# Batch 0 of a fused linear attention and swish layer, laid out as head half x 64 partitions with nine tokens each

## The chip, the cores and the metric

The kernel runs on one core of a Trainium2 chip. The metric is the device time in microseconds (us) of one execution of the whole program. Below, PE is the matrix engine (its weight loads are listed as PEld), DVE the vector engine, ACT the scalar engine with its function tables, POOL the engine that here issues all loads, and SP the engine that issues the stores and DMA transposes.

## What is computed

Linear attention with phi(x) = elu(x) + 1, and behind it a layer of two products with a swish between them. All inputs are float32.

```python
batch, n_heads, seq, head_dim = (8, 8, 576, 64)
d_model, d_ff = (512, 2048)

def phi(x):
    return np.where(x > 0, x, np.exp(x) - 1.0) + 1.0
q_p, k_p = (phi(q), phi(k))
kv = np.einsum('bhsd,bhse->bhde', k_p, v)
z = np.sum(k_p, axis=2)
num = np.einsum('bhsd,bhde->bhse', q_p, kv)
den = np.einsum('bhsd,bhd->bhs', q_p, z)[..., None] + 1e-06
x = (num / den).transpose(0, 2, 1, 3).reshape(B * S, H * D)

h = x @ w_in
g = h * (1.0 / (1.0 + np.exp(-beta * h)))
out = g @ w_out
```

## The kernel before

Everything is computed in bfloat16 with float32 accumulation; the loads convert on the way. The order of work on each engine is the order of the program text: the kernel switches the framework's own scheduling off and writes the order out by hand. Each engine works through its own list and waits where an operand is not ready or a buffer is not free.

**Batches and row blocks.** The eight batches are worked through one after another. The 576 tokens of a batch are four row blocks of 128 (token 4p + j of the first 512 lies on partition p, as block j) and a tail of 64 tokens, which makes the fifth block (`NT` = 5). The tails of all eight batches are gathered in `xT_tail` and form a ninth pass (`b == B`) at the end.

**Attention of one batch.** `exp_` (L203, ACT), `relu` (L210, DVE) and `phi` (L216 a minimum with 1, L217 an addition, DVE) make phi of k and q. `v_copy` (L299) puts v beside columns of ones, so that one product gives kv and z. `kv_mm` (L274) makes kv, 40 products of 64 stationary columns each, `kv_evac` (L284) moves it into a block-diagonal operand `kv_bd`. q is transposed (`q_trans`, L309, on PE for batches 1 and 2, by DMA from batch 3), then `num_mm` (L328) gives numerator and denominator of a row block and `num_norm` (L342 to L344, DVE) divides. `x_trans` (L362) transposes the result into `xT` for batches 0 to 2, a DMA does so from batch 3.

**The two products.** `h_phase` and `h_last` (`h_mm`, L382) multiply by `w_in`, 16 column blocks `ff` of 128, and `silu` (L374, ACT) follows. `y_phase` or `y_phase_wide` (`y_mm`, L422) multiply by `w_out`, and `y_out` and `store` write the rows out. The attention of batch b + 1 is placed among the products of batch b: a dictionary `plan` says behind which group which steps are recorded. `w_out` is loaded in float32 into buffers that are free at the start, and `w_out_scale` (L186 on DVE, L188 on ACT) multiplies it by 1/beta.

**Batch 0** has nothing to hide behind. Its k, q and v are loaded by `load_halves` in two halves of the heads (L118) with one load of the tail tokens between them (L123). For q, `split0` makes the two summands max(x, 0) and exp(min(x, 0)) (L235 to L237), and `q_add0` (L245) transposes both on PE and adds them in PSUM; `q_out0` moves the sum to `qT`. 32 products without a use (`warm`, L490) run on PE while the first loads are under way. The w_in products of batch 0 take row blocks 0 and 1 one by one at first, as these become ready.

**Loads.** All are issued by POOL, in program order, and served by one queue: k, q, v of batch 0, four quarters of `w_in` (L147), k and q of batch 1 (L73, L77), the first half of `w_out` (L112), and then the third quarter of `w_out`, v of batch 1 and the last quarter. Each issue waits until the load eight places before it has landed. PSUM is two pools: `mm` (four banks) and `att` (two pairs of banks); a step that takes a buffer waits for the reader of the one that had it before.

Of the kernel before, what the change touches and what calls it, by code (L numbers as in the profile page):

```python
# [10 lines left out]
BF16 = mybir.dt.bfloat16  # L11
# [5 lines left out]
def kernel(  # L17
# [24 lines left out]
    WARM = 32  # L42
# [71 lines left out]
    def load_halves(dst, src):  # L114

        for i in range(2):
            hs = slice(i * HH, (i + 1) * HH)
            nc.gpsimd.dma_start(  # L118
                out=dst[:, hs, 0:NJ, :].rearrange("p h j d -> p h (j d)"),
                in_=src[0, hs, 0:MAIN, :].rearrange("h (p j) d -> p h (j d)", j=NJ),  # L120
            )
            if i == 0:
                nc.gpsimd.dma_start(  # L123
                    out=dst[0:TAIL, :, NJ, :],
                    in_=src[0, :, MAIN:S, :].rearrange("h s d -> s h d"),
                )
# [4 lines left out]
    nc.vector.memset(g_sb[0][:, 0, :], 0.0)  # L131
    clear_tail(0)
    nc.vector.memset(vraw[0][TAIL:P, :, NJ, :], 0.0)
# [7 lines left out]
    load_halves(xqk[0][:, 1], k)  # L141
    make_identity(nc, identity)
    make_identity(nc, ident16)
    load_halves(xqk[0][:, 0], q)
    load_halves(vraw[0], v)
    for i in range(4):
        nc.gpsimd.dma_start(out=w_in_sb[i], in_=w_in_v[:, :, i * 512 : (i + 1) * 512])  # L147
    load_k(1)
    load_q(1)
    load_w_out(0)  # L150
    load_w_out(1)
# [7 lines left out]
    for i in range(2):  # L159
        nc.vector.memset(vaug[i][:, :, :, D : D + 2], 1.0)  # L160
        nc.vector.memset(vaug[i][TAIL:P, NJ, :, D : D + 2], 0.0)

# [6 lines left out]

    def make_beta():  # L170
        bps = att_banks()[:, 0, 0:FC]
        nc.tensor.matmul(bps, beta_row, ident16, is_transpose=True, start=True, stop=True)
# [33 lines left out]

    def relu(b, a, h0=0, h1=H):
        if h0 == 0:
            st[b, "r", a] = work.tile([P, H, NT, D], BF16, tag="r", name="r")
        nc.vector.tensor_scalar(  # L210
            st[b, "r", a][:, h0:h1], xqk[b % NX][:, a, h0:h1], 0.0, None, ALU.max
        )

    def phi(b, a, h0=0, h1=H):
        e = st[b, "e", a][:, h0:h1]
        nc.vector.tensor_scalar(e, e, 1.0, None, ALU.min)  # L216
        nc.vector.tensor_add(  # L217
            st[b, "p"][:, a].rearrange("p j (h d) -> p h j d", h=H)[:, h0:h1],
            st[b, "r", a][:, h0:h1], e,
        )  # L220

    def split0(h0, h1):


        if h0 == 0:
            st["r0"] = work.tile([P, H, NT, D], BF16, tag="r", name="r")
            st["e0"] = work.tile([P, H, NT, D], BF16, tag="e", name="e", bufs=3)
        x = xqk[0][:, 0, h0:h1]
        e, r = [
            st[a].rearrange("p h j d -> p (h j d)").rearrange(  # L230
                "p (j h d) -> p h j d", j=NT, h=H
            )[:, h0:h1]
            for a in ("e0", "r0")
        ]
        nc.vector.tensor_scalar(e, x, 0.0, None, ALU.min)  # L235
        nc.scalar.activation(e, e, ACTF.Exp)
        nc.vector.tensor_scalar(r, x, 0.0, None, ALU.max)  # L237

    def q_add0(t, bank, p0, p1):
        n = rows(t)  # L240
        for p in range(p0, p1):
            for src in ("r0", "e0"):
                a = st[src].rearrange("p h j d -> p (h j d)")
                c0 = t * DM + p * P
                nc.tensor.matmul(  # L245
                    bank[:, p * P : p * P + n], a[:n, c0 : c0 + P],
                    identity[:n, :n],
                    start=(src == "r0"), stop=(src == "e0"), skip_group_check=True,
                )

    def q_out0(t, bank, dve):
        n = rows(t)
        copy(
            st[0, "qT"][:, t, :, :n],
            bank.rearrange("p (c n) -> p c n", c=KC)[:, :, :n], dve,
        )
# [152 lines left out]

# [258 lines left out]
```

## Time and profile before

| | |
|---|---|
| median of 6 runs | 300.88 us (300.66 to 301.82) |
| the profiled execution | 300.82 us, of which the span from the first to the last instruction is 299.1 us |
| PE busy | 285.5 us, 95% of the span |
| ACT, DVE, POOL busy | 176.0, 134.1 and 54.5 us |
| DMA | 36.44 MB in 71687 packets, 39264 of them under 512 B |
| first product with w_in, first product with w_out | at 20.93 us, at 36.77 us |

All times inside the execution are microseconds from the start of the span, of the one execution that was profiled. A line of the timeline gives the start, the length, the engine, the source line, the operation with its output and inputs, shapes and count, and in brackets how long the engine had been idle before and what ended that. Busy times of PE are modelled from pipelined matrix products, so a product of 512 columns that is listed with 0.38 us follows the one before it after 0.22 us.

### The profile page before, as it was taken

The numbers are of one execution on the slowest core, as the hardware profiler recorded it, in microseconds if no ns is written. First come the engines' busy times: TensorE is split into PE (matmuls) and PEld (weight loads), VectorE is DVE, ScalarE is ACT, GpSimd is POOL, SyncE is SP. The second block draws the span as 40 slices with busy tenths as digits, with TensorE's granted clock in tenths as the row PEclk, the third lists the DMA queues.
The fourth block names the chain that finished last, engine by engine and source line by source line (L and its number), as shares of the span: only waits on it lengthen the run. The fifth ranks groups of instructions, "written<-read, shape, count | busy, mean of one in ns | idle before, by whom it ended". The sixth has DMA issues, their size and how long they took to land.

```text
span 299.1 us, 4767 instructions
## 1 busy us (share of the span) xinstructions
PE 285.5 (95%) x1882; PEld 146.0 (49%) x1903; DVE 134.1 (45%) x260; ACT 176.0 (59%) x235; POOL 54.5 (18%) x71
## 2 busy tenths in 40 slices
PE   3979998999999999999999999999999999999994
PEld 1458445654556454445444544444444444444444
DVE  6773469703678144824482448244825400110012
ACT  3569894889989690769076907690761067007600
POOL 8943564742201400060002000000000000000000
PEclk9999999999999999999999999999999999999999
DMA  7999999999926996399539243224322710020024
GB/s 83 170 207 196 366 300 195 224 223 192 181 69 164 147 146 123 87 137 197 133 84 120 60 127 84 41 61 124 85 40 62 109 52 1 35 72 35 0 55 88
DMA packets 71687, 36.44 MB, mean 122 GB/s; under 512 B 39264, under 2 KB 66160, under 8 KB 71664
## 3 DMA queue, kind: packets, MB, share of 16 engines
q0 software_dynamic: 40944, 20.45, 48.3%
q1 hardware_dynamic: 30560, 15.55, 21.5%
q8 instruction: 15, 0.25, 0.3%
q10 hardware_dynamic: 160, 0.13, 0.2%
q14 instruction: 8, 0.07, 0.1%
HBM read 36.71 MB, written 9.44 MB: 154 GB/s over the span
## 4 chain that ended last, share of the span: by engine, by line
PE 80%; DMA 11%; DVE 3%; POOL 2%; issue 1%; ACT 1%; POOLq 0%
PE mm L382 36%; PE mm L422 36%; DMA vraw<-in_v_dram 6%; DMA xqk<-in_q_dram 5%; PE att L328 3%; PE att L274 2%; PE mm L454 1%; PE att L382 1%; POOL xqk L118 1%; DVE xs L344 1%; PE att L362 1%; ACT q_pT L301 1%; PE att L309 1%; DVE qk_p L217 1%; POOL xqk L123 0%
## 5 line engine op out<-in xcount | busy, mean ns | idle before, releaser
L422 PE MATMUL mm<-w_out,g 128*128 128x512 bf16 x541 | 127.4, 379 | 1.2 <-issue 0.3
L374 ACT ACTIVATE g<-mm,beta_c 128x512 bf16<-128x512 f32 (+2 forms) x156 | 95.2, 633 | 51.7 <-PE mm L382 51.2
L382 PE MATMUL mm<-xT,w_in 128*128 128x512 bf16 (+2 forms) x560 | 107.5, 349 | 0.5 <-ACT xT L301 0.5
L382 PEld LDWEIGHTS <-w_in 128*128 128x128 bf16 x656 | 62.2, 98 | 61.4 <-issue 0.8
L422 PEld LDWEIGHTS <-g 128*128 128x128 bf16 x560 | 52.7, 98 | 57.0
L432 DVE COPY y_sb<-mm 128x512 f32<-128x512 f32 x27 | 18.7, 692 | 70.6 <-PE mm L422 69.1
L203 ACT ACTIVATE e<-xqk 128x2560 bf16<-128x2560 bf16 (+1 forms) x16 | 34.5, 2196 | 5.1 <-DMA xqk<-in_k_dram 5.1
L374 ACT ACT_TABLE_LOAD x6 | 7.7, 1283 | 38.1 <-PE mm L382 38.0
L344 DVE TENSOR_TENSOR xs<-att,rden 128x512 bf16<-128x512 f32 (+1 forms) x40 | 27.6, 690 | 1.4
L217 DVE TENSOR_TENSOR qk_p<-r,e 128x2560 bf16<-128x2560 bf16 (+1 forms) x16 | 22.5, 1409 | 0.5
L73 POOL DMA_DIRECT2D vraw<-in_v_dram x7 | 6.2, 879 | 79.0 <-DVE vaug L299 72.2
L216 DVE TENSOR_SCALAR e<-e 128x2560 bf16<-128x2560 bf16 (+1 forms) x16 | 12.8, 802 | 14.5 <-ACT e L203 14.5
L284 DVE CAST kv_bd<-att 64x260 bf16<-64x260 f32 x16 | 6.8, 426 | 27.0 <-PE att L274 26.8
L342 DVE TENSOR_SCALAR den<-att 128x8 f32<-128x8 f32 (+1 forms) x40 | 6.4, 161 | 27.4 <-PE att L328 27.4
L328 PE MATMUL att<-kv_bd,q_pT 128*128 128x130 bf16 (+1 forms) x160 | 16.1, 222 | 1.0 <-ACT q_pT L301 0.4
L328 PEld LDWEIGHTS <-q_pT 128*128 128x128 bf16 (+1 forms) x160 | 11.7, 100 | 10.7 <-DVE xs L344 2.1
L210 DVE TENSOR_SCALAR r<-xqk 128x2560 bf16<-128x2560 bf16 (+1 forms) x16 | 12.5, 789 | 7.2 <-DMA xqk<-in_k_dram 4.2
L382 PE MATMUL mm<-xT_tail,w_in 128*128 128x512 bf16 x63 | 13.9, 379 | 0.1
L73 POOL DMA_DIRECT2D xqk<-in_k_dram x7 | 9.2, 1319 | 8.9 <-ACT e L203 6.2
L490 PE MATMUL mm<-g,identity 128*128 128x512 bf16 x33 | 9.5, 453 | 0.2 <-issue 0.2
L299 DVE COPY vaug<-vraw 128x2560 bf16<-128x2560 bf16 (+1 forms) x9 | 7.3, 806 | 4.4 <-DMA vraw<-in_v_dram 4.4
L203 ACT ACT_TABLE_LOAD x7 | 9.0, 1283 | 0.1
(76 smaller groups left out, 150.0 us busy)
## 6 DMA issues: line engine op xcount, KB each, us to landing
out_dram<-y_sb SPq DMA_DIRECT2D x32, 256.0 KB, 2.3
xqk<-in_k_dram POOLq DMA_DIRECT2D x7, 512.0 KB, 11.5
xqk<-in_q_dram POOLq DMA_DIRECT2D x7, 512.0 KB, 12.6
vraw<-in_v_dram POOLq DMA_DIRECT2D x7, 512.0 KB, 11.3
w_in<-in_moe_w_in_dram POOLq DMA_DIRECT2D x4, 512.0 KB, 11.7
g<-in_moe_w_out_dram POOLq DMA_DIRECT2D x4, 512.0 KB, 10.6
xqk<-in_moe_w_out_dram POOLq DMA_DIRECT2D x2, 512.0 KB, 14.8
xT<-in_moe_w_out_dram POOLq DMA_DIRECT2D x2, 512.0 KB, 12.5
```

Source lines behind the costliest of these rows:

```text
L73: eng.dma_start(out=dst[:, :, 0:NJ, :].rearrange("p h j d -> p h (j d)"), in_=src[b, :, 0:MAIN, :].rearrange("h (p j) d -> p h (j d)", j=NJ),)
L203: nc.scalar.activation(st[b, "e", a][:, h0:h1], xqk[b % NX][:, a, h0:h1], ACTF.Exp)
L210: nc.vector.tensor_scalar(st[b, "r", a][:, h0:h1], xqk[b % NX][:, a, h0:h1], 0.0, None, ALU.max)
L216: nc.vector.tensor_scalar(e, e, 1.0, None, ALU.min)
L217: nc.vector.tensor_add(st[b, "p"][:, a].rearrange("p j (h d) -> p h j d", h=H)[:, h0:h1], st[b, "r", a][:, h0:h1], e,)
L328: nc.tensor.matmul(nps[:n, p // 2, c0 : c0 + 2 * (D + 1)], st[b, "qT"][:, t, p, :n], kv_bd[b % 2][:, p], start=True, stop=True, skip_group ...
L344: nc.vector.tensor_mul(xs[:n], nv[:, :, :, 0:D], rden[:n, :, :, None].to_broadcast([n, 2, 4, D]))
L374: nc.scalar.activation(g_sb[b % 2][:, ff, c0:c1], hp[:, c0:c1], ACTF.Silu, scale=beta_c[:, ff : ff + 1],)
L382: nc.tensor.matmul(hp[:, c0:c1], w_in_sb[ff // 4][:, kc, (ff % 4) * P : (ff % 4 + 1) * P], x[:, t0:t1, kc, :] if b < B else x[:, kc, c0:c1 ...
L422: nc.tensor.matmul(yp, g_sb[b % 2][:, ff, t * P : (t + 1) * P], w_out_sb[ff // 4][:, ff % 4, :], start=(ff == 0), stop=(ff == FC - 1),)
L432: nc.vector.tensor_copy(y_sb, yp)
L490: nc.tensor.matmul(st["warm"], identity, g_sb[0][:, 0, :], start=True, stop=True, skip_group_check=True,)
```

## The change

- **Layout of batch 0.** Partitions 0 to 63 hold heads 0 to 3, partitions 64 to 127 heads 4 to 7, and partition p of a half holds tokens 9p to 9p + 8 of each head. There is no tail load. Each load is two DMAs of 64 partitions (`load_nine`). The output rows of batch 0 are stored accordingly, 64 rows at a time.
- **Order of loads.** q's tokens 0 to 3 first, then k, two halves of v, and the other five tokens of q. The first half of w_out is issued ahead of k and q of batch 1.
- **Products of batch 0.** k's and v's product (`kv_mm0`) and q's transposes (`q_trans0`) use 64 of the 128 rows of the array, the two head halves in the two row halves, with outputs in different banks. The transposes of q's second part (`q_second`, `q_tail0`) are placed among the w_in products, and so is the numerator of row block 2.
- **phi** is min(exp(x), max(x, 0) + 1) in all batches: `relu` adds 1 in the same instruction, and one minimum of two tensors takes the place of a minimum and an addition.
- **Warm-up products** are 20 at the start, on an operand that needs no identity matrix, and 8, 2, 3 and 4 between steps of batch 0.
- **beta**: the transpose stays early on PE, its five DVE instructions move between the two copies of v.
- Some steps change engine or place: two `x_trans` copies go from ACT to DVE, memsets for later batches (`tidy0`) go behind batch 0's use of the buffers, `w_out_scale(0)` comes earlier in the plan.

```diff
-    WARM = 32
+    WARM = 20
...
+    def load_nine(dst, src, h0=0, h1=HH, j0=0, j1=N9):
+        for g in range(2):
             nc.gpsimd.dma_start(
+                out=dst[g * TAIL : (g + 1) * TAIL, h0:h1, j0:j1, :].rearrange(
+                    "p h j d -> p h (j d)"
+                ),
+                in_=src[0, g * HH + h0 : g * HH + h1, :, :]
+                .rearrange("h (p j) d -> p h j d", j=N9)[:, :, j0:j1, :]
+                .rearrange("p h j d -> p h (j d)"),
+            )
...
-    load_halves(xqk[0][:, 1], k)
+    load_nine(q9, q, j1=4)
+    load_nine(k9, k)
     make_identity(nc, identity)
     make_identity(nc, ident16)
-    load_halves(xqk[0][:, 0], q)
-    load_halves(vraw[0], v)
+    load_nine(v9, v, h1=2)
+    load_nine(v9, v, h0=2)
+    load_nine(q9, q, j0=4)
     for i in range(4):
         nc.gpsimd.dma_start(out=w_in_sb[i], in_=w_in_v[:, :, i * 512 : (i + 1) * 512])
+    load_w_out(0)
+    load_w_out(1)
     load_k(1)
     load_q(1)
-    load_w_out(0)
-    load_w_out(1)
...
-            st[b, "r", a][:, h0:h1], xqk[b % NX][:, a, h0:h1], 0.0, None, ALU.max
+            st[b, "r", a][:, h0:h1], xqk[b % NX][:, a, h0:h1], 0.0, 1.0, ALU.max, ALU.add
...
-        e = st[b, "e", a][:, h0:h1]
-        nc.vector.tensor_scalar(e, e, 1.0, None, ALU.min)
-        nc.vector.tensor_add(
+        nc.vector.tensor_tensor(
             st[b, "p"][:, a].rearrange("p j (h d) -> p h j d", h=H)[:, h0:h1],
-            st[b, "r", a][:, h0:h1], e,
+            st[b, "r", a][:, h0:h1], st[b, "e", a][:, h0:h1], ALU.min,
         )
...
+    def q_trans0(t, banks, c0):
+        for jj in range(2 if t < NJ else 1):
+            for a in range(2):
+                for g in range(2):
+                    gs = slice(g * TAIL, (g + 1) * TAIL)
+                    m0 = c0 + a * P + jj * TAIL
+                    nc.tensor.matmul(
+                        banks[:, g, m0 : m0 + TAIL],
+                        st["p0"][0][gs, 2 * t + jj, 2 * a : 2 * a + 2, :],
+                        identity[gs, gs],
+                        is_transpose=True, start=True, stop=True, skip_group_check=True,
+                    )
...
+    def kv_mm0(a, kvp):
+        for j in range(N9):
+            for g in range(2):
+                gs = slice(g * TAIL, (g + 1) * TAIL)
+                m0 = a * 2 * (D + 1)
                 nc.tensor.matmul(
+                    kvp[:, g, m0 : m0 + 2 * (D + 1)],
+                    st["p0"][1][gs, j, 2 * a : 2 * a + 2, :],
+                    va9[gs, j, 2 * a : 2 * a + 2, 0 : D + 1],
+                    start=(j == 0), stop=(j == N9 - 1), skip_group_check=True,
                 )
...
     begin(0)
-    make_beta()
     st["warm"] = mm_bank([P, 512])
     warm(WARM)
...
+    beta_trans()
...
+    exp0(0, 0, 4)
+    relu0(0, 0, 4)
+    phi0(0, 0, 4)
+    exp0(1, 0, 5)
+    exp0(1, 5, N9)
+    qb = att_banks(BF16)
+    q_trans0(0, qb, 0)
+    q_trans0(1, qb, 256)
+    warm(8)
+    q_out0(0, qb, 0, False)
+    q_out0(1, qb, 256, False)
+    relu0(1, 0, 5)
+    relu0(1, 5, N9)
+    phi0(1, 0, 5)
+    phi0(1, 5, N9)
+    v_copy0(0, 2)
+    make_beta()
+    kvp = att_banks()
+    kv_mm0(0, kvp)
+    warm(2)
+    v_copy0(2, HH)
+    kv_mm0(1, kvp)
+    kv_evac0(kvp)
+    warm(3)
+    num_mm(0, 0)
+    num_mm(0, 1)
+    exp0(0, 4, N9)
+    relu0(0, 4, N9)
     silu_table()
     num_norm(0, 0)
+    warm(4)
+    x_trans(0, 0, dve=True)
+    phi0(0, 4, N9)
     num_norm(0, 1)
...
         {
-            1: [F(x_trans, 0, 1)],
-            2: [F(num_mm, 0, 3), F(num_norm, 0, 3)],
-            5: [F(x_trans, 0, 2), F(num_mm, 0, 4), F(num_norm, 0, 4)],
-            8: [F(x_trans, 0, 3)],
-            12: [F(x_trans, 0, 4)],
-            17: [F(begin, 1), F(relu, 1, 1)],
-            19: [F(relu, 1, 0), F(w_out_scale, 0)],
+            1: [F(q_second)],
+            3: [F(x_trans, 0, 1, dve=True), F(num_mm, 0, 2), F(num_norm, 0, 2)],
+            5: [F(num_mm, 0, 3), F(num_norm, 0, 3)],
+            6: [F(q_tail0)],
+            7: [F(x_trans, 0, 2)],
+            9: [F(x_trans, 0, 3)],
+            10: [F(num_mm, 0, 4), F(num_norm, 0, 4), F(tidy0)],
+            14: [F(x_trans, 0, 4)],
+            17: [F(w_out_scale, 0)],
+            19: [F(begin, 1), F(relu, 1, 1), F(relu, 1, 0)],
         },
```

## The prediction

> **What bounds the kernel now.** I read the page first, then the busy times by stage, then the first 21 us and the stretch from 43 to 51 us instruction by instruction. The stages (stretch and its length, then busy us of PE, PEld, DVE, ACT, POOL, granted clock, DMA share, GB/s):
>
> ```profile
> 4.50:20.93 16.43, 14.31 (x131) 7.98 (x133) 11.65 (x30) 9.01 (x11) 12.29 (x15) 1.00 1.35 177
> 20.93:26.58 5.65, 5.58 (x72) 4.85 (x72) 2.81 (x8) 5.18 (x15) 1.90 (x3) 1.00 1.31 203
> 26.58:36.70 10.12, 10.12 (x65) 6.06 (x65) 3.76 (x7) 9.15 (x16) 5.40 (x7) 1.00 1.30 306
> 44.00:57.00 13.00, 11.45 (x125) 6.67 (x125) 11.44 (x25) 8.07 (x14) 6.89 (x9) 1.00 1.53 205
> 57.00:254.00 197.00, 195.79 (x1259) 97.15 (x1272) 91.18 (x167) 124.23 (x157) 20.61 (x24) 1.00 0.66 112
> ```
>
> After 20.93 us, where the first product with w_in starts, PE is busy all the time but for 1.55 us between 44 and 57 us and some 1.2 us in the 197 us behind. So a change can win only two things: an earlier 20.93, and that 1.55. Whatever it adds to PE behind 20.93 is paid in full. Every DVE instruction that it takes from batches 2 to 7 (the minimum in phi, 0.84 us each) is worth nothing by itself: DVE is busy 91 of 197 us there, PE 195.8.
>
> The head, from the timeline (start, length, instruction):
>
> ```profile
> 6.09 1.27 ACT L203 ACTIVATE e<-xqk 128x1280 bf16<-128x1280 bf16 x1 [3.85 <-DMA xqk<-in_k_dram]
> 8.57 1.27 ACT L203 ACTIVATE e<-xqk 128x1280 bf16<-128x1280 bf16 x1 [1.21 <-DMA xqk<-in_k_dram]
> 10.40 0.83 DVE L217 TENSOR_TENSOR qk_p<-r,e 128x1280 bf16<-128x1280 bf16 x1
> 14.43 0.49 DVE L299 COPY vaug<-vraw 128x1280 bf16<-128x1280 bf16 x1 [1.16 <-DMA vraw<-in_v_dram]
> 15.68 0.70 DVE L299 COPY vaug<-vraw 128x1280 bf16<-128x1280 bf16 x1 [0.76 <-DMA vraw<-in_v_dram]
> 16.44 0.51 PE L274 MATMUL att<-vaug,qk_p 128*64 128x65 bf16 x20 [0.96 <-DVE vaug L299]
> 16.98 0.87 DVE L284 CAST kv_bd<-att 64x260 bf16<-64x260 f32 x2 [0.60 <-PE att L274]
> 18.00 0.40 PE L328 MATMUL att<-kv_bd,q_pT 128*128 128x130 bf16 x4 [0.28 <-ACT q_pT L301]
> 20.93 0.61 PE L382 MATMUL mm<-xT,w_in 128*128 128x128 bf16 x8 [0.45 <-ACT xT L301]
> ```
>
> The second half of v, landing at 15.68, ends last; k was there at 8.57. Behind v everything is a chain: copy, 20 products, eviction, numerator, normalisation, transpose, first product with w_in. And the later stall:
>
> ```profile
> 43.77 1.15 DVE L299 COPY vaug<-vraw 128x2560 bf16<-128x2560 bf16 x1 [2.46 <-DMA vraw<-in_v_dram]
> 44.84 0.97 DVE L216 TENSOR_SCALAR e<-e 128x2560 bf16<-128x2560 bf16 x1
> 45.16 0.82 PE L274 MATMUL att<-vaug,qk_p 128*64 128x65 bf16 x40 [0.46 <-ACT g L374]
> 45.85 1.49 DVE L217 TENSOR_TENSOR qk_p<-r,e 128x2560 bf16<-128x2560 bf16 x1
> 47.40 0.62 PE L309 MATMUL att<-identity,qk_p 128*128 128x128 bf16 x8 [0.44 <-DVE qk_p L217]
> ```
>
> Batch 1's v lands at 43.77, and q's transposes wait for copy, minimum and addition on DVE.
>
> **The change, part by part.** The sum is made against the profiled execution's own 300.82 us (span 299.1, 1.72 around it). The median of the runs is 300.88, 0.06 more.
>
> *Loads.* The first part of q (262 KB as bf16) now has the place and the bytes of k's first half, so it lands at about 6.09. All of k (590 KB) follows in pieces of 1152 B instead of 512 and 128 B. Rates seen: w_in, in pieces of 1024 B, ran at 205 GB/s (16 to 20 us), the pieces of batch 0 at 144 (6 to 9 us), a mixture at 185 (12 to 14 us). So k lands at 6.09 + 590/205 = 8.97 at best and 6.09 + 590/144 = 10.19 at worst; I take 185: 9.3, since k's new pieces are nearer to w_in's but POOL still issues beside them. Here a rule speaks against the change: the Trainium skill, "DMA: Bandwidth & Descriptors", Rules for kernel authors, says two transfers to disjoint partition halves serialize, and asks for one transfer over 128 partitions. By it the split of every load into two 64-partition DMAs brings nothing of itself, and the sum would keep the rate of 144; this trace has no load split so. Ten issues of some 0.72 us and 0.9 us for the identities end near 9.8, ahead of their data. The w_in issues behind them wait for landings (k, v) that come before POOL reaches them.
>
> *The chain of batch 0.* v (two pairs of 295 KB behind k) lands by 9.3 + 590/185 = 12.5 and no longer ends last; k does, through ACT and DVE in this order. Two exponentials, 1280 and 1024 columns: 1.27 + 1.06, to 11.65. The last minimum (1024 columns, 0.83 x 0.8): 12.4. Copy of half of v (1152, 0.49 x 0.9): 12.85. The five beta instructions, which now stand between the two copies and took 1.08 at 4.87 to 5.95: 13.95. Second copy: 14.4. Eighteen products of 130 columns: 0.057 each when alone (numerators run four in 0.23), about 0.02 less if the two row halves overlap as the two column halves of L274 do (40 in 0.82); I take 0.75 and 0.15 of latency: 15.3. Eviction 0.87: 16.2. From evicted kv to normalised rows before: 17.85 to 19.60, 1.75: 17.95; q's relu (0.49) falls beside the numerator. Transpose 0.39, its copy on DVE 0.42 (between 0.29 for 256 and 0.69 for 1024 columns), handovers 0.15: the first product with w_in starts at 18.9, 2.0 us earlier. Bounds: k at 8.97 and products overlapped fully, 2.6 earlier; k at 10.19, products serial (1.03), and both copies at 0.70 as at 15.68 instead of 0.49, 0.5 earlier. w_in's first quarter must be there: before it was issued ninth and its successor on POOL moved at 18.53; now all of batch 0 is through about 1.5 us sooner, so it is.
>
> *What moves behind the start.* Before, all transposes of q and three numerators were done by 20.93. Now 16 + 4 transposes (q_second, q_tail0) and one more numerator stand among the w_in products. A 64-row transpose costs 0.033 when in a row, 0.055 with what surrounds four of them (0.22 in the chain), so 0.66 to 1.1; the numerator 0.35. I take 1.2. PE also waits: xT of the second row block is ready only after DVE has done phi of q's second part (0.83), a normalisation (1.1), a q copy and an xT copy (0.42 each) and handovers, 2.9 us behind the first xT, while PE has 0.89 of products, 0.7 of transposes and 0.58 of x_trans and numerator to do, 2.2: a wait of 0.7 (0.3 to 1.1). The same stretch before held 0.35 of slack (5.65 less 13 groups at 0.22 or 0.43, three transposes at 0.23, two numerators at 0.35 = 5.30). Net 1.2 + 0.7 - 0.35 = 1.55 later. So the products with w_out, from 36.77 before, start 0.45 earlier.
>
> *Stall from 44 to 57.* The shorter phi takes 0.97 us from DVE between v's copy and q's transposes, and v comes some 1 us sooner as the earlier loads are through. PE's wait of 0.44 and the 0.16 behind it go; the wait before L274 (0.46) stays, since it hangs on ACT's silus in the two banks, which move with the rest. I take 0.4 (0 to 0.9): numerators then wait for ACT's q copies.
>
> *Without price.* w_out ahead of batch 1: w_out's first quarter came at 33.97 and its four scalings ended by 36.2, just ahead of 36.77. Batch 0 is through at 6.09 + 1508/185 = 14.2 (15.68 before), w_in (2.1 MB) 10.2 later, four pieces of w_out at 1.34 each (33.97 to 35.31) by 29.8, then k and q of batch 1 at 590/205 = 2.9 each: 32.7 and 35.6. Their exponentials start at 35.5 and 37.8 before: covered by some 2 us, less the 0.45; beyond that, every us late is one more at the silus behind. tidy0 (1.1 us of memsets) and eight stores of half size for batch 0 lie where DVE and SP idle. Fewer warm-ups: they fill idle PE.
>
> Sum: -2.0 + 1.55 - 0.4 = -0.85: 299.97, by the median 300.0.
>
> **Rivals.** (1) *The first loads stay slow.* If batch 0's pieces flow at 144 GB/s whatever their length, k lands at 10.19, the start is only 0.8 earlier with serial products and 0.6 with one slow copy, 1.55 is added behind, 0.1 comes back: +0.85, 301.7. It decides from k landing after about 10.15, where the sum is nought. For it: 135 to 158 GB/s held from 3 to 12 us; against: w_in's 205. (2) *The gain is eaten.* What is saved ahead is paid inside the w_in products, and the later stall is ACT's anyway: 300.9, within 0.6. (3) *All goes well*: k at 205 GB/s, row halves overlapped, stall 0.7 smaller: -2.6 + 1.2 - 0.7 = -2.1, 298.7. (4) *The clock.* PE idles from the end of the eight warm-ups (near 10) to the first products (12.9). The 32 warm-ups took 9.10 us, nine of them until 8.58, 0.43 each, the others 0.23: a relapse would cost up to 1.9 us, 301.9. The Trainium skill, "TensorE: Matmul & The Clock Gate", Part 1, puts the relapse at an idle window of about 3.4 us. Idle stretches of 1 us here did no harm.
>
> **How the numbers follow.** Within 0.2% (0.6 us, about what a measurement can tell) counts as the same. My forecast 0.38, (3) 0.14: faster 0.52. (2) 0.18. (1) 0.23 and (4) 0.07: slower 0.30. Range from the unknown costs together: best 298.3, worst 302.6; 298.6 to 302.0 leaves out two in ten.
>
> **What would show it.** First w_in product near 18.9 (right: 18.3 to 19.6), exponential of k near 9.3, first w_out product near 36.3, PE busy in the 13 us around the kv products of batch 1 for over 11.8. Wrong if k's exponential starts after 10.2, if matmuls of 512 columns take 0.43 again behind 10 us, or if w_out products start after 37.

## The result, and the profile after

The changed kernel takes 301.97 us (median of 20 runs, 300.99 to 302.81); the kernel before, run beside it on the same chips, 300.93. The ratio is 1.0034 [1.0025, 1.0042]: slower by a third of a per cent, a little more than a measurement can tell. The forecast was 300.0, faster than before; 301.97 lies at the far end of the range that it gave (298.6 to 302.0), on the other side of the kernel before. The profiled execution of the changed kernel took 302.81 us, with a span of 301.0; it is the slowest of the 20, so the stages below show the loss somewhat larger than the median has it (span +1.9, median +1.04).

The stages of the changed kernel, from the busy times by stretch. The columns are the stretch, its length, then busy us and instructions of PE, PEld, DVE, ACT and POOL, the granted clock, the share of the DMA engines and GB/s:

```profile
4.50:21.77 17.27, 12.94 (x94) 6.54 (x94) 7.89 (x21) 7.00 (x8) 11.78 (x17) 0.80 1.19 188
21.77:29.96 8.19, 7.70 (x105) 6.19 (x104) 6.17 (x19) 6.37 (x17) 3.02 (x5) 1.00 1.13 330
29.96:39.28 9.32, 9.32 (x58) 5.27 (x58) 4.97 (x10) 8.36 (x14) 5.89 (x7) 1.00 1.42 250
46.50:59.48 12.98, 11.70 (x131) 7.28 (x130) 8.62 (x23) 8.63 (x15) 5.83 (x8) 1.00 1.57 195
59.48:256.40 196.92, 195.68 (x1257) 96.65 (x1269) 81.69 (x154) 126.03 (x156) 18.24 (x22) 1.00 0.62 108
```

The first line is the head: it ends 0.84 us later than before (21.77 against 20.93), and its granted clock is 0.80 where it was 1.00. (The record of the clock begins at 6.81 us here and at 8.90 in the kernel before; the warm-ups ahead of that took 0.43 us each in both.) The last is the bulk of the kernel: 196.92 us, within a hundredth of before when the stretch is cut at the same instructions (57.59 to 254.50, 196.91), although DVE is busy 9 us less in it. So everything is decided in the first 59 us. The head, from the timeline (start, length, engine and line, operation, count, and in brackets the idle time before and what ended it):

```profile
5.31 1.06 ACT L252 ACTIVATE e<-xqk 128x1024 bf16<-128x1024 bf16 x1 [3.07 <-DMA xqk<-in_q_dram]
8.89 1.90 PE L562 MATMUL mm<-g 128*128 128x512 bf16 x8
10.91 2.21 ACT L252 ACTIVATE e<-xqk 128x1280 bf16<-128x1280 bf16 x2 [4.54 <-DMA xqk<-in_k_dram]
14.28 1.16 PE L301 MATMUL att<-vaug,qk_p 64*128 64x130 bf16 x18 [3.48 <-DVE vaug L292]
15.14 0.40 DVE L292 COPY vaug<-vraw 128x1152 bf16<-128x1152 bf16 x1
17.43 1.46 PE L562 MATMUL mm<-g 128*128 128x512 bf16 x3
21.77 0.61 PE L443 MATMUL mm<-xT,w_in 128*128 128x128 bf16 x8 [0.51 <-DVE xT L360]
39.28 1.03 PE L495 MATMUL mm<-w_out,g 128*128 128x512 bf16 x4
```

q's first part comes early (5.31), but k only at 10.91, and ACT has stood idle for 4.54 us. PE's eight warm-ups end at 10.79; it then idles for 3.48 us, until v's first half has been copied behind k's phi on DVE (14.28). From there on it is slow: three warm-ups of 512 columns take 1.46 us, some 0.4 each behind the first, and eight took 1.90 before the gap, 0.22 each behind the first. The clock by stretches (columns as above):

```profile
12.00:14.00 2.00, 0.00 (x0) 0.09 (x1) 1.66 (x3) 2.00 (x4) 2.00 (x4) 0.91 1.31 199
14.00:16.00 2.00, 1.39 (x19) 1.02 (x19) 1.40 (x7) 0.61 (x2) 2.00 (x4) 0.50 1.25 206
18.00:20.00 2.00, 2.00 (x13) 1.14 (x11) 1.47 (x5) 0.26 (x2) 1.17 (x1) 0.50 1.24 206
21.00:22.00 1.00, 0.49 (x10) 0.36 (x8) 0.70 (x2) 0.00 (x0) 0.45 (x1) 1.00 1.24 206
```

The record of the clock has half clock from 13.64 to 20.46 us, over the kv products and the numerators of the first row blocks (e1's expectation has these two times 0.24 too late). Two faults thus lie on top of each other: k is late, and the wait for it costs the clock.

The later stall is better than before. PE around batch 1's kv products and q's transposes:

```profile
47.66 0.82 PE L335 MATMUL att<-vaug,qk_p 128*64 128x65 bf16 x40 [0.45 <-ACT g L435]
48.65 0.81 PE L495 MATMUL mm<-w_out,g 128*128 128x512 bf16 x3 [0.16 <-issue]
49.29 1.06 PE L370 MATMUL att<-identity,qk_p 128*128 128x128 bf16 x16
51.93 0.40 PE L389 MATMUL att<-kv_bd,q_pT 128*128 128x130 bf16 x4 [0.49 <-ACT q_pT L362]
```

The sixteen transposes run in a row, without the two waits of 0.44 and 0.16 us; the wait for ACT's silu ahead of the kv products is still there (0.45).

### The profile page after: what moved, and what is told of

It is laid out like the page before. It is cut to its first block, busy times and chain, and to the rows that moved or that the text cites. A ratio compares the mean times of both kernels' runs of the same rounds, so it can differ in the third digit from the quotient of the medians.

```text
span 301.0 us, 4706 instructions
## 1 busy us (share of the span) xinstructions
PE 288.3 (96%) x1877; PEld 146.3 (49%) x1898; DVE 123.4 (41%) x248; ACT 176.1 (59%) x232; POOL 52.8 (18%) x72
## 4 chain that ended last, share of the span: by engine, by line
PE 81%; ACT 8%; issue 4%; DMA 3%; DVE 2%; POOL 1%; ACTq 0%; POOLq 0%
PE mm L443 39%; PE mm L495 33%; PE att L389 3%; DMA xqk<-in_k_dram 3%; ACT e L225 2%; PE att L335 2%; PE mm L527 1%; PE mm L562 1%; ACT g L435 1%; ACT L225 1%; ACT L435 1%; ACT q_pT L362 1%; ACT w_out L210 1%; PE att L301 1%; ACT e L252 1%
## 5 line engine op out<-in xcount | busy, mean ns | idle before, releaser
L435 ACT ACTIVATE g<-mm,beta_c 128x512 bf16<-128x512 f32 (+2 forms) x156 | 97.4, 632 | 92.5 <-PE mm L443 92.2
L225 ACT ACTIVATE e<-xqk 128x2560 bf16<-128x2560 bf16 x14 | 31.9, 2329 | 0.1
L238 DVE TENSOR_TENSOR qk_p<-r,e 128x2560 bf16<-128x2560 bf16 x14 | 20.9, 1490 | 14.6 <-ACT e L225 13.9
L345 DVE CAST kv_bd<-att 64x260 bf16<-64x260 f32 x14 | 6.0, 427 | 37.5 <-PE att L335 37.4
L389 PEld LDWEIGHTS <-q_pT 128*128 128x128 bf16 (+1 forms) x160 | 12.2, 103 | 10.9 <-DVE xs L405 2.1
L562 PE MATMUL mm<-g 128*128 128x512 bf16 x36 | 12.7, 514 | 1.6 <-DVE g L145 1.2
L233 DVE TENSOR_SCALAR r<-xqk 128x2560 bf16<-128x2560 bf16 x14 | 11.4, 818 | 4.1 <-DMA xqk<-in_q_dram 2.5
L73 POOL DMA_DIRECT2D xqk<-in_k_dram x7 | 7.1, 1019 | 15.9 <-ACT e L225 9.1
L252 ACT ACTIVATE e<-xqk 128x1024 bf16<-128x1024 bf16 (+1 forms) x4 | 4.5, 1158 | 9.0 <-DMA xqk<-in_k_dram 4.5
L73 POOL DMA_DIRECT2D xqk<-in_q_dram x7 | 8.2, 1170 | 5.9 <-DMA w_in<-in_moe_w_in_dram 1.8
L404 DVE RECIPROCAL rden<-den 128x8 f32<-128x8 f32 (+1 forms) x40 | 8.1, 201 | 1.4
## 6 DMA issues: line engine op xcount, KB each, us to landing
w_in<-in_moe_w_in_dram POOLq DMA_DIRECT2D x4, 512.0 KB, 10.2
```

What stands on the lines that cost most here:

```text
L73: eng.dma_start(out=dst[:, :, 0:NJ, :].rearrange("p h j d -> p h (j d)"), in_=src[b, :, 0:MAIN, :].rearrange("h (p j) d -> p h (j d)", j=NJ),)
L225: nc.scalar.activation(st[b, "e", a][:, h0:h1], xqk[b % NX][:, a, h0:h1], ACTF.Exp)
L233: nc.vector.tensor_scalar(st[b, "r", a][:, h0:h1], xqk[b % NX][:, a, h0:h1], 0.0, 1.0, ALU.max, ALU.add)
L238: nc.vector.tensor_tensor(st[b, "p"][:, a].rearrange("p j (h d) -> p h j d", h=H)[:, h0:h1], st[b, "r", a][:, h0:h1], st[b, "e", a][:, h0: ...
L389: nc.tensor.matmul(nps[:n, p // 2, c0 : c0 + 2 * (D + 1)], st[b, "qT"][:, t, p, :n], kv_bd[b % 2][:, p], start=True, stop=True, skip_group ...
L404: nc.vector.reciprocal(rden[:n], den[:n])
```

## The experiments

The table has the landmarks of each kernel's profiled execution, in us: the rate of the loads from 3 to 6 us (GB/s), the start of k's first exponential (of both halves of k where there are two, in the kernel before and e8), the first product with w_in, the first product with w_out, the second group of batch 1's `x_trans` products on PE, and the span. "Median" is that of all runs, and the ratio is to the kernel before on the same chip; kernels without a ratio have a single run.

| kernel | 3 to 6 us | k | w_in | w_out | x_trans | span | median | ratio |
|---|---|---|---|---|---|---|---|---|
| before | 135 | 6.09, 8.57 | 20.93 | 36.77 | 54.09 | 299.1 | 300.93 | |
| changed | 145 | 10.91 | 21.77 | 39.28 | 55.98 | 301.0 | 301.97 | 1.0034 |
| e1_hold_clock | 152 | 10.83 | 20.20 | 37.70 | 54.41 | 299.4 | 300.80 | 0.9993 |
| e2_beta_early | 122 | 10.12 | 20.32 | 37.82 | 54.53 | 299.5 | 301.83 | 1.0027 |
| e3_hold_beta | 130 | 10.25 | 19.36 | 36.87 | 53.57 | 298.6 | 300.56 | 0.9985 |
| e4_hold_old_phi | 134 | 10.09 | 19.65 | 37.15 | 53.85 | 298.9 | 300.74 | 0.9995 |
| e5_hold_old_order | 137 | 10.07 | 19.75 | 37.25 | 53.95 | 299.0 | 301.24 | 1.0008 |
| e8_before_phi_order | 136 | 6.04, 8.48 | 20.76 | 38.76 | 54.95 | 299.9 | 303.66 | 1.0095 |
| e9_k_first | 179 | 7.12 | 17.20 | 34.70 | 51.91 | 296.9 | 298.71 | 0.9929 |
| e10_w_in_first | 156 | 13.79 | 23.29 | 40.80 | 57.50 | 302.5 | 304.44 | |
| e12_full_width | 90 | 15.44 | 26.07 | 43.58 | 60.28 | 305.3 | 307.09 | 1.0213 |
| e13_q_whole | 185 | 10.97 | 21.26 | 38.76 | 55.47 | 300.5 | 302.26 | |
| e14_k_first_only | 187 | 6.59 | 17.15 | 34.65 | 52.47 | 297.5 | 298.82 | 0.9933 |
| e15_q_heads_lead | 143 | 10.22 | 21.50 | 39.00 | 55.71 | 300.7 | 302.50 | |
| e16_k_quarters | 139 | 7.84 | 18.58 | 36.09 | 53.77 | 298.8 | 300.58 | |

### The clock and the beta instructions

**e1_hold_clock**: sixteen more warm-ups fill the idle time.

```diff
-    warm(8)
+    warm(24)
```

> The changed kernel with 24 warm-up products instead of 8 between q's transposes and the kv products, so that PE has no idle stretch before 14.3 us. Theory A: the clock fell at 13.88 us because PE stood idle from 10.8 to 14.28, and the half clock until 20.7 cost the chain some 1.5 us (2 warm-ups at 0.43, kv products, 3 and 4 warm-ups, numerators). Then every product of 512 columns after 9 us takes 0.22, the first w_in product comes at 19.8 to 20.4 instead of 21.77, and the time is 300.6 to 301.1, ratio to before 0.999 to 1.001, without the spread of 301.0 to 302.8 between runs. Theory B: the late k (10.91) and the work moved behind the start explain all; the extra warm-ups only fill a wait: first w_in product at 21.5 or later, ratio 1.003.

300.80 us, 0.9993 [0.9981, 1.0005]. The same two instructions that took 1.16 us and started the w_in products at 21.77, from the timeline of this kernel:

```profile
14.50 0.69 PE L301 MATMUL att<-vaug,qk_p 64*128 64x130 bf16 x18 [1.36 <-DVE vaug L292]
20.20 0.61 PE L443 MATMUL mm<-xT,w_in 128*128 128x128 bf16 x8 [0.52 <-DVE xT L360]
```

k is as late as in the changed kernel (10.83), so the 1.57 us between 21.77 and 20.20 are the clock's. By the medians it is 1.17. In none of the changed kernel's runs was the mean granted clock above 0.994, in none of this one's below 0.997. With the clock held, the change is worth nothing: no faster and no slower than the kernel before.

**e2_beta_early** and **e3_hold_beta**: the five DVE instructions on beta stand ahead of k's steps instead of between the two copies of v, once without and once with the 24 warm-ups.

```diff
     phi0(0, 0, 4)
+    make_beta()
     exp0(1, 0, 5)
...
     v_copy0(0, 2)
-    make_beta()
```

> The changed kernel with the five beta instructions on DVE ahead of k's phi (where DVE stands idle from 7.1 to 10.9 us) instead of between the two copies of v. Theory A: the second copy ends 1.0 us earlier (14.6 instead of 15.54) but PE is then still busy with the first products and two warm-ups at half clock until 16.2, so nothing is won: 0 to -0.2 us against the changed kernel, ratio 1.003. Theory C: the beta instructions are on the path that sets the start, as the prediction's sum has them: -0.8 to -1.0 us, ratio 1.000.

> Both edits together: 24 warm-ups and beta early. Theory A: with the clock up PE is through with the first products and two warm-ups at about 15.3 to 15.7, so the copy at 14.6 instead of 15.54 wins 0 to 0.3 us over the kernel with the clock held alone: ratio 0.998 to 1.000. Theory C: 0.8 to 1.0 us over it: ratio 0.996 to 0.998.

e2: 301.83, 1.0027 [1.0014, 1.0041]; e3: 300.56, 0.9985 [0.9973, 0.9996]. Without the warm-ups PE idled 4.21 us and the clock fell (0.986 to 0.994 over the runs): an edit that shortens a chain behind a late landing gains nothing that can be seen as long as the clock falls. With them, the move is worth some 0.2 us by the medians; the two intervals overlap, and k lay 0.6 earlier in e3's trace than in e1's, so its own worth is not settled. In e2's trace the half clock lasted 3.41 us only, although PE had idled for longer than in the changed kernel; the last section comes back to that.

### phi and the order of w_out

**e4_hold_old_phi** is e1 with the old phi (maximum; minimum with 1; addition) for batches 1 to 7.

```diff
...
-        nc.vector.tensor_tensor(
+        e = st[b, "e", a][:, h0:h1]
+        nc.vector.tensor_scalar(e, e, 1.0, None, ALU.min)
+        nc.vector.tensor_add(
```

> The changed kernel with 24 warm-ups, and for batches 1 to 7 the phi of before (maximum, minimum, addition). Batch 0 keeps the new one. Theory H: the shorter phi is what shortened the stretch from the first w_out product to batch 1's w_in products (20.82 before, 20.20 after), so it comes back: first kv products of batch 1 to q's transposes later by 0.4 to 0.6, time 301.2 to 301.4 against 300.80 with the new phi. Theory I: v of batch 1 lands sooner as the earlier loads are through sooner, and DVE has some 2 us in hand before q's transposes: no difference, 300.7 to 300.9.

300.74, 0.9995 [0.9983, 1.0008]. The shorter phi is worth nothing in the time, and not even in the stall it was meant for. From the timeline of this kernel, phi of batch 1's q on DVE and q's transposes on PE:

```profile
43.77 0.81 DVE L239 TENSOR_SCALAR e<-e 128x2560 bf16<-128x2560 bf16 x1
44.62 1.49 DVE L240 TENSOR_TENSOR qk_p<-r,e 128x2560 bf16<-128x2560 bf16 x1
47.17 1.06 PE L372 MATMUL att<-identity,qk_p 128*128 128x128 bf16 x16
```

The long phi ends at 46.1, the transposes want it at 47.17: v was copied at 42.86, 0.9 earlier than before, and the long phi is done 1.06 us ahead of the transposes.

**e5_hold_old_order** is e1 with the first half of w_out issued behind k and q of batch 1 again, as before.

```diff
+    load_k(1)
+    load_q(1)
     load_w_out(0)
     load_w_out(1)
-    load_k(1)
-    load_q(1)
```

> The changed kernel with 24 warm-ups, and w_out's first half behind k and q of batch 1 again. The order is hidden by both theories if w_out's four scalings on DVE end before the first w_out product at 37.7: first quarter at about 33, scalings to 35.3, no difference, 300.7 to 300.9. Rival: w_out's second half then lands after 37 and its scalings stand in front of phi and v's copy on DVE, which delays q's transposes: 0.3 to 0.8 slower.

301.24, 1.0008 [0.9991, 1.0024]: 0.4 above e1 and 0.3 above the expected range by the medians, but the two intervals overlap. In its trace the stretch from the first w_out product to the second `x_trans` is 16.70 us as in e1 (16.71) and e4 (16.70), against 17.32 before. Either of the two edits can go, and the 0.62 us stay; no run takes both away.

**e8_before_phi_order** is the kernel before with the new phi and with the loads of w_out's first half ahead of batch 1's k and q, nothing else.

> The kernel before with only two parts of the change: phi as min(exp(x), max(x,0)+1) in batches 1 to 7, and w_out's first half ahead of k and q of batch 1. Batch 0 is as before, so v of batch 1 lands at about 43.8 again. Theory H: DVE is through with q's phi 0.9 sooner, PE's wait of 0.44 ahead of q's transposes and what follows it go: 300.3 to 300.6, ratio 0.998 to 0.999. Theory I: no difference, since the shorter time comes from the earlier loads: 300.9, ratio 0.9995 to 1.0005.

303.66 (301.65 to 305.78), 1.0095 [1.0059, 1.0132], which neither theory had. The kernel had moved the loads only: on DVE the four scalings of w_out's first quarter still stood behind the maximum of k and of q, and these two now landed later. DVE and PE in this kernel's timeline:

```profile
37.48 0.83 DVE L210 TENSOR_SCALAR r<-xqk 128x2560 bf16<-128x2560 bf16 x1 [2.33 <-DMA xqk<-in_q_dram]
38.22 1.67 DVE L186 TENSOR_SCALAR w_out<-xqk,rbeta 128x512 bf16<-128x512 f32 x4
38.76 3.41 PE L420 MATMUL mm<-w_out,g 128*128 128x512 bf16 x14 [1.99 <-DVE w_out L186]
```

PE stood for 1.99 us before a w_out whose first quarter had landed by 28.6. In this profiled run the clock held (1.00, 301.65 us, the fastest); in the six others the mean clock was 0.994 or 0.989, so some half clock came on top; where, no profile of them shows. What the change has right here is that `w_out_scale(0)` moved up with its load: at 30.38 in the changed kernel, ahead of both maxima.

### Why k is late

**e10_w_in_first**: two quarters of w_in are issued ahead of batch 0.

```diff
+    nc.gpsimd.dma_start(out=w_in_sb[0], in_=w_in_v[:, :, 0:512])
+    nc.gpsimd.dma_start(out=w_in_sb[1], in_=w_in_v[:, :, 512:1024])
     load_nine(q9, q, j1=4)
     load_nine(k9, k)
...
-    for i in range(4):
+    for i in range(2, 4):
```

> The changed kernel with the first two quarters of w_in issued ahead of q and k: the same 1024-byte pieces over 128 partitions that ran at 205 GB/s at 16 to 20 us, now first in the queue. Its time is not the question (all of batch 0 comes later, some 4 us slower); the rate between 4 and 8 us is. Theory D: the first loads of an execution are slow whatever their pieces: 140 to 165 GB/s. Theory E: batch 0's own pieces (or their two halves of 64 partitions) are slow: 195 GB/s or more for w_in there, and the 150 appear where q and k are moved.

The busy times by stretch, columns as above:

```profile
4.00:6.00 2.00, 2.00 (x6) 0.71 (x5) 0.00 (x0) 0.00 (x0) 1.91 (x6) 1.00 1.23 205
6.00:9.00 3.00, 2.52 (x11) 0.93 (x9) 0.00 (x0) 0.00 (x0) 1.94 (x4) 1.00 1.23 200
9.00:12.00 3.00, 0.00 (x0) 0.00 (x0) 0.43 (x1) 1.06 (x1) 1.83 (x3) 1.00 1.31 202
```

Both theories fall. The first microseconds are not slow in themselves (205 GB/s from 4 us on), and the pieces of q and k are not slow in themselves either: from 9 us on they flowed at 202.

**e9_k_first**: k is loaded and worked on ahead of q's first part, q's transposes move behind the kv products, the beta instructions are early, and 18 warm-ups stand ahead of the kv products.

```diff
+    load_nine(k9, k)
     load_nine(q9, q, j1=4)
-    load_nine(k9, k)
...
-    exp0(0, 0, 4)
-    relu0(0, 0, 4)
-    phi0(0, 0, 4)
     exp0(1, 0, 5)
     exp0(1, 5, N9)
...
+    exp0(0, 0, 4)
+    make_beta()
...
+    warm(18)
```

> The changed kernel with k's load ahead of q's first part, the exponentials and phi of k ahead of those of q, q's transposes behind the kv products, beta early and the clock held by 18 warm-ups ahead of the kv products. Theory F: k's landing sets the start (10.2 to 10.9 us behind q, 8.5 to 8.9 when first), so the kv products start near 12.3 instead of 13.92 (clock held and beta early), and the first w_in product comes at 18.2 to 18.6, then held by w_in's first quarter, which lands near 18.2: 299.3 to 299.9, ratio 0.995 to 0.997. Theory G: v's second half or ACT's q copies end last instead: first w_in product at 19.2 or later, no gain over 300.56.

298.71 us, 0.9929 [0.9910, 0.9947], better than either theory and than both kernels. **e14_k_first_only** takes the extra warm-ups and the early beta away again and keeps the order alone, that of the loads and that of the work on k and q.

> The kernel with k loaded and processed first (298.71), but with the eight warm-ups of the changed kernel in place of 18, and the five beta instructions back between the two copies of v. TensorE is then idle from about 9.1 to 11.3 us, 2.2 us in place of 3.5. Theory A, the clock falls only when TensorE has idled for longer than that: the granted clock stays at full, the beta instructions cost 0 to 0.5 us since the second half of v comes at 12.2, 298.7 to 299.3 us. Rival, any idle stretch of over 2 us there brings the half clock: the first kv products of 18 take 1.16 us instead of 0.69, 299.9 to 300.6 us.

298.82 us, 0.9933 [0.9915, 0.9951]: the order alone does it, 3.15 us below the changed kernel. Stretch and timeline of this kernel:

```profile
3.00:6.00 3.00, 3.00 (x11) 1.11 (x10) 0.53 (x4) 0.00 (x0) 2.85 (x9) 1.00 1.15 187
6.59 3.21 ACT L252 ACTIVATE e<-xqk 128x1280 bf16<-128x1280 bf16 x3 [4.35 <-DMA xqk<-in_k_dram]
11.08 0.69 PE L301 MATMUL att<-vaug,qk_p 64*128 64x130 bf16 x18 [1.41 <-DVE vaug L292]
17.15 0.61 PE L443 MATMUL mm<-xT,w_in 128*128 128x128 bf16 x8 [0.52 <-DVE xT L360]
```

The loads flow at 187 GB/s in place of 145, k is there 4.3 us sooner, and PE idles 1.41 us in place of 3.48, and the clock stays. (The rival in the expectation needed a gap of over 2 us and was not tested here; e16 below has one.) The w_in products start 3.78 us earlier than in the kernel before; 1.66 of this are given back by the moved transposes (17.50 from there to the w_out products, 15.84 before) and 0.50 around batch 1's kv products, where PE now waits 0.79 us for ACT's silu.

**e13_q_whole** has all of q ahead of k, in pieces of 1152 bytes, and 30 warm-ups; **e15_q_heads_lead** is e14 with two heads of q (two transfers of 147 KB, pieces of 1152 bytes) ahead of k.

```diff
-    load_nine(q9, q, j1=4)
+    load_nine(q9, q)
     load_nine(k9, k)
```

```diff
+    load_nine(q9, q, h1=2)
     load_nine(k9, k)
-    load_nine(q9, q, j1=4)
```

> The changed kernel with 30 warm-ups, and q of batch 0 loaded whole, in pieces of 1152 bytes, ahead of k (no first part of four tokens in pieces of 512 bytes, no second part). One look, for the rates. Theory P, the pieces of 512 bytes of q's first part slow the queue: from 3 to 6 us it flows at 170 GB/s or more as in the kernel with k first (169, 199, 168), and k is there by 10.0 though 330 KB more lie ahead of it. Theory O, the pieces have nothing to do with it: 135 to 160 GB/s from 3 to 6 us, k's exponential at 11.5 to 13. The time is above 301 in both, since k is later than in the kernel with k first.

> The kernel with k processed first and eight warm-ups (298.82), but loaded in another order: a first part of q leads again, now two heads of nine tokens in place of four tokens of four heads, 295 KB in pieces of 1152 bytes in place of 262 KB in pieces of 512; then k, v and the other two heads of q. One look, for the rates and for k's landing. Theory P, what slows the first microseconds of the changed kernel is that its leading transfer consists of pieces of 512 bytes: here 3 to 6 us flow at 165 GB/s or more, and k's exponential starts by 9.3 although 295 KB lie ahead of it. Theory O, any part of q ahead of k does it: 3 to 9 us at 140 to 160 GB/s, k's exponential at 10.2 to 11.0. q's second part lands behind v, so the time is above 299.5 in both.

The stretch from 3 to 6 us, first of e13, then of e15:

```profile
3.00:6.00 3.00, 3.00 (x9) 1.07 (x8) 0.53 (x4) 0.00 (x0) 2.86 (x9) 1.00 1.17 185
```

```profile
3.00:6.00 3.00, 3.00 (x9) 1.04 (x8) 0.53 (x4) 0.00 (x0) 2.85 (x9) 1.00 0.97 143
```

e13 has the rate that theory P asked for, though k came at 10.97 and not by 10.0: there was a dip to 106 GB/s from 6 to 7 us, where the queue goes over from q to k. Even so k landed at the same time as in the changed kernel with 330 KB more ahead of it. But e15 goes to theory O: the same long pieces, and 143 GB/s, k at 10.22. So it isn't the length of the pieces. What e9, e13 and e14 share is that the first two transfers have 295 KB each, in e10 524 KB; in the changed kernel and in e15 they have 131 and 147 KB.

**e16_k_quarters** puts that to the test: e14 with k in four transfers of two heads, same order, same pieces, same bytes.

```diff
-    load_nine(k9, k)
+    load_nine(k9, k, h1=2)
+    load_nine(k9, k, h0=2)
     load_nine(q9, q, j1=4)
```

> The kernel with k processed first and eight warm-ups (298.82), with k of batch 0 loaded in four transfers of two heads (147 KB each, 64 partitions, pieces of 1152 bytes as before) in place of two of 295 KB; k still leads and nothing else is moved, but two more issues on POOL put everything behind k some 1.3 us later. One look, for the rates. Theory T, the size of the first transfers sets the rate of the first microseconds: 3 to 6 us flow at 120 to 160 GB/s as with two heads of q ahead (143), and k's exponential starts at 7.5 or later. Theory U, what slows is that another tensor leads k: 175 GB/s or more from 3 to 6 us, the exponential at 6.5 to 7.2 as with k in two transfers.

```profile
3.00:6.00 3.00, 3.00 (x11) 1.17 (x10) 0.53 (x4) 0.00 (x0) 2.86 (x9) 1.00 1.01 139
7.84 3.17 ACT L253 ACTIVATE e<-xqk 128x1280 bf16<-128x1280 bf16 x3 [5.60 <-DMA xqk<-in_k_dram]
11.51 1.09 PE L302 MATMUL att<-vaug,qk_p 64*128 64x130 bf16 x18 [2.05 <-DVE vaug L293]
```

Theory T by its numbers: 139 GB/s in place of 187, and k 1.25 us later, in one run. The edit halves the leading transfers; it also makes two issues more, which puts all that stands behind k later. Behind the dip, from 6 to 9 us, the rate is 189.

Half microseconds show that it is a dip and not a slow queue. Two rows of e15, then two of e13:

```profile
4.00:4.50 0.50, 0.50 (x2) 0.15 (x1) 0.00 (x0) 0.00 (x0) 0.38 (x3) 1.00 1.06 164
4.50:5.00 0.50, 0.50 (x2) 0.15 (x1) 0.00 (x0) 0.00 (x0) 0.48 (x2) 1.00 0.58 83
```

```profile
5.50:6.00 0.50, 0.50 (x3) 0.22 (x2) 0.00 (x0) 0.00 (x0) 0.50 (x2) 1.00 1.22 173
6.00:6.50 0.50, 0.50 (x4) 0.22 (x3) 0.00 (x0) 0.00 (x0) 0.50 (x2) 1.00 0.93 85
```

In e15 and e16 the rate falls at 4.5 us (to 83 and 97), when about the 295 KB of the first pair of transfers have been moved; in e13, whose first pair has 590 KB, it falls at 6.0, outside the window from 3 to 6 us. From 3 to 9 us the rates lie closer together: 181 (e14), 173 (e13), 164 (e16), 152 (e15), 149 (changed). So a large first pair moves the dip back, and with k as that pair k is there before it (behind k the rate falls to 155 only in e14, to 145 in e9); why the queue dips there, and why less behind k, is open.

**e12_full_width** was to try the other suspicion, that transfers over half the partitions are slow: k and v of batch 0 head by head, each over all 128 partitions, with 24 warm-ups.

> The changed kernel with the 24 warm-ups; of batch 0, k and v are loaded head by head, each transfer over all 128 partitions (the lower 64 from one half of the heads, the upper 64 from the other), in place of two transfers of 64 partitions; k takes four issues in place of two, some 1.3 us more of POOL, v still four. Compare with the 300.80 of the same kernel with two transfers of 64 partitions. Theory H, the 64-partition halves are what makes batch 0's loads slow (145 to 155 GB/s from 3 to 9 us): the rate from 4 to 9 us rises to 180 or more, k's exponential of 1280 columns starts by 9.8, the first product with w_in by 19.3, about 299.9 us. Theory S, the halves cost nothing: the rate from 4 to 9 us stays below 165, k's exponential starts at 10.5 to 11.5 and the first product with w_in at 20.0 to 21.0, 300.6 to 301.6 us.

307.09 us, 1.0213 [1.0188, 1.0238], outside both. It doesn't answer its question, since the transfers fell apart into small packets, as the DMA view of the first 14 us shows; k came at 15.44, PE idled for 5.51 us and the clock fell as well (0.986 to 0.989).

```profile
DMA packets 5741, 1.04 MB, mean 74 GB/s; under 512 B 4562, under 2 KB 5741, under 8 KB 5741
```

Whether one transfer over 128 partitions with long pieces would be faster is open.

## Why the prediction was wrong, point by point

Two steps failed; the others held within a few tenths.

1. **k's landing was mis-sized: 9.3 forecast, 10.91 found, outside the bounds of 8.97 and 10.19.** The term adds bytes divided by a rate to the landing of q's first part. The rate was too high, 185 GB/s against 145 (3 to 6 us) and 154 (6 to 9), but q's part came early (5.31, forecast 6.09), and 5.31 + 590/154 = 9.14: the two nearly cancel. What failed is the step from bytes to landing, that k is there once the queue has moved as many bytes as stand up to k's end. Those are 0.85 MB, and the DMA view has them moved by 8.5 us, while 1.29 MB were moved before k's exponential started:

```profile
DMA packets 1113, 0.86 MB, mean 101 GB/s; under 512 B 74, under 2 KB 1113, under 8 KB 1113
DMA packets 1533, 1.29 MB, mean 119 GB/s; under 512 B 118, under 2 KB 1533, under 8 KB 1533
```

(0 to 8.5 and 0 to 10.9 us.) The trace marks the landing of each transfer sixteen times. For k's second transfer fifteen marks lie between 7.79 and 9.55 us and the last at 10.83, when fifteen of the sixteen marks of v's first transfer, issued behind it, had come. In all six kernels with this order of loads (the changed kernel, e1 to e5) these marks spread over 2.0 to 3.0 us, and k's exponential started between 10.07 and 10.91; all six lie far past 9.3, and three past 10.19, the worst case. Where k leads in two transfers they spread over 0.25 us (e14) and 0.80 (e9). What holds the last packets back is open: being behind another load is not enough, since in e10, behind two quarters of w_in, the spread was 0.43.

2. **The clock was a rival at 7 in 100, and it came in every run.** I had the gap from about 10 to 12.9 us, 2.9 long, and set it against a rule of an idle window of about 3.4. But 2.05 us were enough in e16, and the gap hung on k's landing, which the same text called uncertain by 1.2 us: with k at 10.19 the gap passes 3.4. The two rivals were one case, and I added them as if they were independent. (The mean granted clock was 0.986 to 0.994 in every run of the changed kernel.) Its price of up to 1.9 us was sound (1.57 in the traces of e1 and the changed kernel, 1.17 in the medians).

3. **The chain behind k was right.** From k's exponential to the second copy of v I had 14.4 - 9.3 = 5.1 and it was 15.54 - 10.91 = 4.63; from there to the first w_in product 4.5, and with the clock held some 4.3 (e1, 15.87 to 20.20). The products' row halves overlap as I took it: 18 in 0.69 us at full clock, 0.75 in the sum. The account of the head is then 18.9 + 1.61 (k) - 0.47 (to v's second copy) + 1.73 (from there, at half clock) = 21.77.

4. **What moved behind the start: 1.55 forecast, 1.67 found** (17.51 from the first w_in to the first w_out product, 15.84 before). e1, e9 and e14 have 17.50 too. The sixteen 64-row transposes took 0.41 us in place of the 0.53 in a row that I had; PE stood idle for 0.49 us between 21.77 and 29.96, 0.07 between 20.93 and 26.58 before: net 0.42, where I had 0.35.

5. **The stall: -0.4 forecast, -0.62 found,** but for the other reason. I gave the gain to the shorter phi together with v's earlier landing. e4 keeps the old phi and has the same 16.70 us, so the shorter phi isn't needed for it.

6. **What had no price had none:** w_out's first quarter was scaled from 30.38 on, the w_out products waited for nothing but the w_in products before them, and the 197 us behind didn't change.

All three signs of being wrong came: k's exponential after 10.2, matmuls of 512 columns at some 0.4 us behind 10 us, w_out's products after 37. Of the rivals, (1) had k's late landing and the slow rate, though with q's part at 5.31 its 144 GB/s would have had k at 9.4, and (4) had the right addition. (1) alone, which is e1, gave no difference where I had 301.7: with the w_in products at 20.20, 0.73 earlier, 1.66 is added and 0.62 comes back, +0.3 in the span; I had let only 0.1 come back. More was to be had than rival (3) hoped for, by an order that I did not consider: with k first the w_in products begin 3.78 us sooner, where my best case was 2.6.

The rule cited against the change (the Trainium skill, "DMA: Bandwidth & Descriptors", Rules for kernel authors: transfers to two partition halves serialize) is neither shown nor refuted, since e12 didn't test it. The same page's account of a transfer issued from GpSimd ("Anatomy of one DMA") gives each transfer a fixed part of about 2.0 us beside its bytes; no run here shows it, since the transfers overlap: in e16 parts of 131 and 147 KB flowed at 189 GB/s from 6 to 9 us. The other rule ("TensorE: Matmul & The Clock Gate", Part 1) names a free-running window of 3413 ns. The traces agree with its length: half clock lasted 6.83 us in the changed kernel (13.64 to 20.46) and in e15, 3.41 in e2, e10 and e16. They disagree with reading it as a free allowance of 3.4 us of idleness, as I did: in e16 an idle stretch of 2.05 us was enough (the last section has the working).

## What to carry to other kernels

Where the first compute of a kernel waits for its first loads, let the largest operand of the longest chain lead, in few large transfers; here a piece of 295 KB put in front (e15) delayed k by 3.6 us, where its bytes make 1.6 at 187 GB/s. Don't take a load as landed when its bytes should have passed: its last packets can come later than packets of loads behind it. Price a wait on a matrix engine twice, once for its length and once for the clock it may lose, and treat both as one case with whatever makes the wait uncertain. When a load is moved ahead of others, move its consumer ahead in the in-order engine's list as well (e8: 1.99 us).

## What the hardware showed that I had not expected

- **A dip behind the first transfers, and late last packets.** Same tensor, order and pieces: two transfers of 295 KB first, 187 GB/s from 3 to 6 us; four of 147 KB, 139, with a dip to 97 behind the first two. Why is not settled: the median packet of 1152 bytes took 107 ns from 3 to 6 us in both, but the mean was 111 in the one and 131 in the other, so some packets are held up. The size of the first transfers isn't the whole rule either, since the kernel before, with k whole in front but in pieces of 512 and 128 bytes, had 135.
- **The clock follows steps of 3.41 us, not the length of a gap.** Behind the warm-ups, every stretch of half clock in these heads lasted 3.41 or 6.83 us. Laid out in steps of 3.41 us from where the clock changes, PE's busy time separates the cases: after a step with 2.05 us of idleness or more (2.05 in e16, 2.73 in e2, 2.74 in e10, 2.85 in the changed kernel, 2.93 in e15, 3.41 in e12) the next ran at half clock; after one with 1.61 or less (1.61 in e2, 1.51 in e10, 1.41 in e14, 1.36 in e1) it did not. At half clock, a step with 0.42 or less brought the full clock back, and one with 0.61 or more (0.61 in e15, 0.97 in the changed kernel, 1.10 in e12) did not. The steps of the changed kernel, then of e2:

```profile
10.22:13.64 3.42, 0.57 (x3) 0.17 (x2) 2.13 (x4) 2.73 (x4) 2.76 (x5) 1.00 1.27 197
13.64:17.05 3.41, 2.44 (x33) 1.74 (x35) 1.76 (x8) 2.00 (x3) 2.87 (x4) 0.50 1.24 206
17.05:20.46 3.41, 3.41 (x24) 1.77 (x19) 2.38 (x6) 1.21 (x2) 1.17 (x1) 0.50 1.24 207
```

```profile
7.78:11.19 3.41, 1.80 (x8) 0.60 (x7) 1.48 (x6) 1.07 (x1) 2.18 (x3) 1.00 1.18 177
11.19:14.61 3.42, 0.69 (x18) 0.72 (x20) 2.56 (x4) 2.12 (x4) 3.42 (x6) 1.00 1.28 197
14.61:18.02 3.41, 3.35 (x27) 1.72 (x27) 1.35 (x3) 2.75 (x3) 1.49 (x3) 0.50 1.24 207
```

  So e2's gap of 4.21 us cost one step, where the changed kernel's 3.48 cost two, and in e2 the clock fell when PE had been at work again for 0.8 us. Where the steps begin differs from trace to trace, so it is partly luck whether a gap of 2 to 3 us costs the clock: e8's 1.99 us lay across two steps in its trace (1.04 and 0.95), and the clock held there, while its other runs show a lower mean. This is read from the traces; no run moved a gap against the steps.
- **Two row halves at once.** Eighteen products of 130 columns on 64 rows took 0.69 us at full clock, sixteen 64-row transposes 0.41, in the two row halves by turns; the change of tiling between them and the products around cost nothing that the timeline shows.
